# Folding a transform by halves and re-ordering three stages of a spectral-filter kernel

## The chip, the cores and the metric

One NeuronCore of one Trainium2 chip. The metric is device time in microseconds (us) of one execution. Times are quoted as the median of the runs of one round series. A profile shows one execution and has its own span, some 1.7 to 2.1 us shorter than the time of that same execution; stage lengths below are read from profiles.

## The reference

```python
def _A_ref(x, w_r, w_i):
    B, S, D = x.shape                        # 1, 2048, 576
    X = rfft2(x.astype(float32), axes=(-2, -1))
    X = X * (w_r + 1j * w_i)                 # weights 2048 x 289
    return irfft2(X, s=(S, D), axes=(-2, -1)).astype(bfloat16)

def _B_ref(x, w_gate, w_up, w_down):         # 576 -> 4608 -> 576
    return (gelu(x @ w_gate) * (x @ w_up)) @ w_down

h  = A_x + _A_ref(layernorm(A_x), w_r, w_i)
h2 = h + _B_ref(layernorm(h), w_gate, w_up, w_down)
```

Everything is bfloat16 in and out. The spectral filter (first line) takes the first 66 us of the kernel; the gated feed-forward (second line) takes the other 430 us.

## The kernel before

The work runs in four stages. The *table stage* computes the layernorm's statistics and multiplies x with a small table along the sequence, giving `U`. The *filter stage* runs, for each of 16 groups, a transform along d (`st_D`), a combination of even and odd parts (`st_U`), a second transform along the sequence (`st_B`), the product with the weights (`st_T`), its sums (`st_Z`), and a transform back (`st_V`). The *inverse stage* finishes the inverse transform and takes the second layernorm. Then comes the *feed-forward*. In the traces each engine does its own steps in the order in which the source issues them.

The parts (cuts are marked):

```python
    # ---- table stage: statistics of a tile by ScalarE are turned into a variance by VectorE
    def ln1_var(i):
        ...
            if c in ACT_TILES:
                P.op(DVE, lambda v, c=c: v.scalar_tensor_tensor(TM[:, 0, c:c + 1], SA[:, 0, c:c + 1], 1.0 / (D * D),
                                                                SA[:, 0, c:c + 1], op0=ALU.mult, op1=ALU.mult), ...)
        ...
                P.op(DVE, lambda v, c=c: v.scalar_tensor_tensor(MV1[:, c, 1:2], SA[:, 1, c:c + 1], 1.0 / D,
                                                                TM[:, 0, c:c + 1], op0=ALU.mult, op1=ALU.subtract), ...)

    TILES = (slice(0, 256, 2), slice(256, 512, 2), slice(1, 256, 2), slice(257, 512, 2), slice(512, D))
    def a_mm(i, k):                       # one matmul per tile of d and of the sequence
        ...
            P.op(PE, ... t.matmul(bank(b, 0, w, o, o + 128), XO[:, c, TILES[k]], ATS[:, c, :], start=True, stop=True), ...)

    # warm-up: loads ScalarE's table with the square root before anything else is there
    P.op(ACT, lambda a: a.activation(SA[:, 0, 0:1], EPT[:, 0:1], ACTF.Sqrt), ...)
    idle_mm(11, 0)
    act_sum(1)
    ...

    # ---- filter stage
    def st_D(i):
        ...                               # even-d result evicted by ScalarE to ES, odd-d result stays in PSUM
    def st_U(i):                          # VectorE: sum and difference from PSUM
        P.op(DVE, ... v.tensor_tensor(CUS[:, s3, :, 0:HK], e2, o2, op=ALU.add), ...)
        ...
        P.op(DVE, ... v.tensor_tensor(CUS[:, s3, :, K2 - 1:HK - 1:-1], e2[:, :, 0:HK - 1], o2[:, :, 0:HK - 1], op=ALU.subtract), ...)
    def st_B(i):                          # 6 matmuls a group, eviction by ScalarE to YS
        ...
    def st_T(i, t_, q0=0, q1=KW, hs=(0, 1)):   # two products a group, 580 elements each
        ...
    def st_V(i):                          # 3 column tiles a group: 128, 128 and the 33 that remain
        ...
    for i in range(NG):                   # GpSimd negates one plane of the weights
        P.op(POOL, lambda v, g=GORD[i]: v.tensor_scalar(WS[:, g, 0, :], WS[:, g, 2, :], -1.0, None, op0=ALU.mult), ...)
    for i in range(NG):
        st_D(i)
        st_U(i)
        if i >= 2:
            st_B(i - 2)
            st_T(i - 2, 0)
            st_T(i - 2, 1)
        if i >= 4:
            st_V(i - 4)
    ...
    # ---- inverse stage: the root of the variance is a power on GpSimd
        P.op(POOL, ... g.tensor_tensor(RS2[:, c0:c1], RS2[:, c0:c1], EXQ[:, c0:c1], op=ALU.pow), ...)
```

## Time and profile before

The kernel takes 498.09 us (498.00 to 498.15, 4 runs).

| Stage, cut at TensorE's first matmul of the next | us | TensorE busy | VectorE busy | ScalarE busy | GpSimd busy |
|---|---|---|---|---|---|
| wait for input | 3.67 | 2.37 | 0.00 | 1.49 | 2.91 |
| table | 16.28 | 13.14 | 14.65 | 15.53 | 4.79 |
| filter | 33.09 | 32.62 | 31.79 | 27.50 | 16.45 |
| inverse | 12.85 | 11.83 | 9.80 | 9.93 | 6.78 |
| feed-forward | 430.11 | 427.79 | 141.78 | 98.83 | 8.71 |

The table is this view of windows of the kernel before, whose row for 0.00 to 3.67 us is left out here. Its columns are the stretch in us, its length, then the busy time of each engine with the number of instructions in brackets, the granted clock, the DMA share and its rate.

```profile
core 0: us, PE busy (x) PEld busy (x) DVE busy (x) ACT busy (x) POOL busy (x), PEclk, DMA share, GB/s
3.67:19.95 16.28, 13.14 (x100) 7.35 (x98) 14.65 (x61) 15.53 (x45) 4.79 (x7) 0.90 0.95 284
19.95:53.04 33.09, 32.62 (x295) 26.42 (x296) 31.79 (x85) 27.50 (x49) 16.45 (x18) 1.00 0.52 161
53.04:65.89 12.85, 11.83 (x101) 8.52 (x102) 9.80 (x33) 9.93 (x22) 6.78 (x11) 1.00 1.02 349
65.89:496.00 430.11, 427.79 (x3825) 242.33 (x3824) 141.78 (x260) 98.83 (x177) 8.71 (x11) 1.00 0.13 38
```

A busy sum near the length of the stage says that an engine *could* be its limit. In the filter two engines qualify, TensorE and VectorE. Which of them is the limit is asked of the chain of waits, followed back from the end (window 36 to 53 us). Each row is a start, a length, and what the end had to wait for; the first line gives the shares of that window by line of the source.

```profile
by line: DVE TP L671 26.5%; PE PS L695 18.1%; issue 14.8%; DVE CUS L645 13.0%; DVE ZS L676 12.4%; DVE CUS L642 4.8%; PE PS L661 3.9%; DVE ZS L671 3.9%; DVE V L702 2.6%; PE PS L712 0.7%
...
41.42 0.74 DVE TP L671 x2
42.16 0.07 DVE CUS L642
42.23 0.22 issue
42.45 0.38 DVE ZS L676
42.83 0.44 DVE CUS L645
43.27 0.74 DVE TP L671 x2
...
```

Until 48.4 us every row is VectorE (DVE) or the gap between two of its instructions: products (TP), sums (ZS), and the sum and difference from PSUM (CUS), group after group. VectorE sets the pace of the filter. (The rows from 24 to 36 us are of the same kind.)

The costliest groups of the filter, from the profile's page (line, engine, operation, output and inputs, shape, count | busy us, mean ns | idle before, and what ended it):

```profile
L716 POOL TENSOR_SCALAR WS<-WS 128x290 bf16<-128x290 bf16 x16 | 15.9, 995 | 9.7 <-DMA WS<-in_A_w_i_dram 8.6
...
L671 DVE TENSOR_TENSOR TP<-YS,WS 128x580 bf16<-128x580 bf16 (+2 forms) x32 | 13.3, 453 | 0.3 <-issue 0.3
...
L664 ACT ACTIVATE YS<-PS 128x578 bf16<-128x578 f32 x16 | 10.5, 655 | 3.5 <-PE PS L661 3.1
L661 PE MATMUL PS<-CUS,BT 128*128 128x289 bf16 (+2 forms) x96 | 10.7, 247 | 0.3 <-DVE CUS L645 0.3
```

GpSimd needs 995 ns to negate 290 elements.

### The profile page before, as it was taken

How to read it: one execution, taken by the hardware profiler on the slowest of the kernel's cores; microseconds unless marked ns; L12 is line 12 of the kernel's file. 1: busy time of each engine (PE TensorE's matmuls, PEld its weight loads, DVE VectorE, ACT ScalarE, POOL GpSimd, SP SyncE). 2: the span in 40 equal slices, each digit the busy share in tenths (PEclk: the TensorE clock that was granted, in tenths of full speed). 3: DMA queues.
4: the chain of work that ended last, by engine and by line, in shares of the span. 5: the costliest groups of instructions: out<-in, count | busy, mean ns of one | idle time of the engine just before them, and what ended most of it. 6: DMA issues, size and time to landing. Idle time of an engine off the chain costs nothing.

```text
span 496.0 us, 9895 instructions
## 1 busy us (share of the span) xinstructions
PE 487.7 (98%) x4323; PEld 285.5 (58%) x4323; DVE 198.0 (40%) x436; ACT 153.3 (31%) x291; POOL 39.6 (8%) x52
## 2 busy tenths in 40 slices
PE   7999999999999999999999999999999999999998
PEld 2688744444488854444477744444677544444775
DVE  6899753343365543433311143433211233333111
ACT  7888763323322223323300023233100133233000
POOL 3644251000000020000000000000000000000000
PEclk9899999999999999999999999999999999999999
DMA  8765798511000052100000001100000000000000
GB/s 284 168 189 205 251 343 278 203 27 26 6 13 13 14 184 68 23 9 1 1 14 19 18 15 23 21 1 1 7 12 19 13 1 1 1 1 2 12 19 19
DMA packets 27163, 31.32 MB, mean 63 GB/s; under 512 B 11664, under 2 KB 19984, under 8 KB 27120
## 3 DMA queue, kind: packets, MB, share of 16 engines
q1 hardware_dynamic: 24224, 18.75, 13.1%
q0 software_dynamic: 2896, 11.95, 7.0%
q8 instruction: 34, 0.56, 0.5%
q14 instruction: 9, 0.07, 0.1%
HBM read 26.35 MB, written 2.36 MB: 58 GB/s over the span
## 4 chain that ended last, share of the span: by engine, by line
PE 89%; DVE 7%; issue 2%; DMA 1%; ACT 1%; POOL 0%; DVEq 0%
PE PS L910 56%; PE PS L960 29%; DVE TP L671 2%; DVE ST L472 1%; DVE CUS L645 1%; PE PS L927 1%; PE PS L775 1%; DVE ZS L676 1%; PE PS L695 1%; PE PS L814 1%; DMA XO<-in_A_x_dram 1%; PE PS L632 1%; DVE U L537 0%; DVE HN L842 0%; PE PS L941 0%
## 5 line engine op out<-in xcount | busy, mean ns | idle before, releaser
L910 PE MATMUL PS<-HT,WG 64*128 64x512 bf16 x2106 | 228.5, 376 | 0.0
L910 PEld LDWEIGHTS PS<-HT,WG 64*128 64x128 bf16 x2106 | 102.2, 94 | 124.8 <-issue 0.9
L920 DVE TENSOR_TENSOR AT<-GL,PS 128x512 bf16<-128x512 bf16 x144 | 99.1, 688 | 176.0 <-ACT GL L919 176.0
L919 ACT ACTIVATE GL<-PS 128x512 bf16<-128x512 f32 x144 | 86.0, 597 | 263.0 <-PE PS L910 249.6
L960 PE MATMUL PS<-WD,AT 128*128 128x288 bf16 (+2 forms) x1152 | 144.2, 286 | 0.0
L960 PEld LDWEIGHTS PS<-WD,AT 128*128 128x128 bf16 x1152 | 110.8, 98 | 30.7 <-ACT GL L919 1.3
L963 DVE TENSOR_TENSOR OS<-PS,XO 128x288 bf16<-128x288 f32 (+2 forms) x32 | 14.6, 458 | 100.3 <-PE PS L960 100.3
L910 PE MATMUL PS<-HT,WGX 64*128 64x512 bf16 x486 | 53.4, 376 | 0.0
L910 PEld LDWEIGHTS PS<-HT,WGX 64*128 64x128 bf16 x486 | 23.7, 94 | 28.8
L716 POOL TENSOR_SCALAR WS<-WS 128x290 bf16<-128x290 bf16 x16 | 15.9, 995 | 9.7 <-DMA WS<-in_A_w_i_dram 8.6
L632 PE MATMUL PS<-FT,U 128*128 128x290 bf16 x96 | 14.4, 287 | 0.4 <-DVE U L537 0.4
L805 ACT ACTIVATE JD<-XO 128x576 bf16<-128x576 bf16 x8 | 5.5, 683 | 28.5 <-DVE XO L944 28.5
L695 PE MATMUL PS<-VT,ZS 128*128 128x256 bf16 x102 | 13.5, 272 | 0.0
L671 DVE TENSOR_TENSOR TP<-YS,WS 128x580 bf16<-128x580 bf16 (+2 forms) x32 | 13.3, 453 | 0.3 <-issue 0.3
L833 POOL TENSOR_TENSOR RS<-RS,EXQ 128x2 f32<-128x2 f32 (+2 forms) x4 | 4.2, 1060 | 113.3 <-DVE RS L831 113.3
L708 ACT ACTIVATE V<-PS 128x768 bf16<-128x768 f32 x15 | 12.0, 811 | 0.9 <-PE PS L695 0.6
L664 ACT ACTIVATE YS<-PS 128x578 bf16<-128x578 f32 x16 | 10.5, 655 | 3.5 <-PE PS L661 3.1
L661 PE MATMUL PS<-CUS,BT 128*128 128x289 bf16 (+2 forms) x96 | 10.7, 247 | 0.3 <-DVE CUS L645 0.3
L632 PEld LDWEIGHTS PS<-FT,U 128*128 128x128 bf16 x96 | 9.2, 98 | 2.9 <-issue 0.6
L842 DVE TENSOR_SCALAR HN<-XO,TM,RS 128x576 bf16<-128x576 bf16 (+1 forms) x32 | 10.4, 372 | 0.4 <-POOL RS L833 0.4
L515 PE MATMUL PS<-ZD 128*128 128x512 bf16 x24 | 9.1, 537 | 1.3 <-POOL ZD L406 1.3
L695 PEld LDWEIGHTS PS<-VT,ZS 128*128 128x128 bf16 x102 | 9.2, 98 | 1.8 <-DVE ZS L676 0.2
(74 smaller groups left out, 199.4 us busy)
## 6 DMA issues: line engine op xcount, KB each, us to landing
WD<-in_B_w_down_dram POOLq DMA_DIRECT2D x9, 576.0 KB, 13.8
WG<-in_B_w_up_dram SPq DMA_DIRECT2D x4, 1152.0 KB, 6.5
WG<-in_B_w_gate_dram POOLq DMA_DIRECT2D x4, 1152.0 KB, 9.2
out_dram<-OS SPq DMA_DIRECT2D x30, 72.0 KB, 1.6
XO<-in_A_x_dram SPq DMA_DIRECT2D x3, 576.0 KB, 7.3
WGX<-in_B_w_up_dram SPq DMA_DIRECT2D x1, 1152.0 KB, 5.9
WGX<-in_B_w_gate_dram POOLq DMA_DIRECT2D x1, 1152.0 KB, 7.6
HT<-HN SPq DMA_TRANSPOSE x60, 2.4
```

The costliest lines, as they stand in the source:

```text
L632: P.op(PE, lambda t, b=b, o=o, dt=dt, us=us, g=g: t.matmul(bank(b, 0, 128, 0, 2 * HK), U[:, us, g, :, :], FT[:, o, dt, :], start=(dt == 0) ...
L661: P.op(PE, lambda t, b=b, tb=tb, pl=pl, q0=q0, q1=q1, m=m, s3=s3, sp_=sp_: t.matmul(bank(b, 0, 128, q0, q1), BT[:, sp_, tb, :], CUS[:, s3, ...
L664: P.op(ACT, lambda a, sl=sl, b0=b0: a.activation(YS[:, sl, :, 0:K2], banks(b0, 2, K2), ACTF.Copy), r=[("PS", b0), ("PS", b0 + 1)], w=[("Y" ...
L671: P.op(DVE, lambda v: v.tensor_tensor(out, YS[:, sl, :, q0:q1], WS[:, g, w_, q0:q1], op=ALU.mult), r=[("Y", sl), ("Wn", i), "Yz", "Zz"] + ...
L695: P.op(PE, lambda t, b=b, o=o, zp=zp, lhs=lhs, sp_=sp_, m=m, n=len(parts): t.matmul(bank(b, 0, 128, o, o + 256), lhs, VT[:, sp_, zp, :], s ...
L708: P.op(ACT, lambda a, dst=dst, src=src: a.activation(dst, src, ACTF.Copy), r=[("PS", bs[0]), ("PS", bs[2])], w=[("V", g, c) for c in range ...
L716: P.op(POOL, lambda v, g=GORD[i]: v.tensor_scalar(WS[:, g, 0, :], WS[:, g, 2, :], -1.0, None, op0=ALU.mult), r=[k for k in wkeys[0 if 1 <= ...
L910: op = P.op(PE, lambda t, h0=h0, kt=kt, wt=wt, b=b, s=(not second and j == 0), e=(second and j == n - 1): t.matmul(bank(b), wg_tile(slot)[ ...
L919: P.op(ACT, lambda a: a.activation(GL[:, s2, :], bank(b0), ACTF.Gelu_apprx_tanh), r=[("PS", b0)], w=[("GL", s2)])
L920: P.op(DVE, lambda v: v.tensor_tensor(AT[:, f, :], GL[:, s2, :], bank(b0 + 1), op=ALU.mult), r=[("GL", s2), ("PS", b0 + 1)], w=[("AT", f)])
L960: P.op(PE, lambda t, b=b, d0=d0, d1=d1, f=f, p=p: t.matmul(bank(b, 0, 128, 0, d1 - d0), AT[:, f, 128 * p:128 * p + 128], WD[:, f, d0:d1], ...
L963: P.op(DVE, lambda v, b=b, d0=d0, d1=d1, p=p, c=c: v.tensor_tensor(OS[:, p % 2, d0:d1], bank(b, 0, 128, 0, d1 - d0), XO[:, c, d0:d1], op=A ...
```

## The change

The intent, part by part:

- **Fold by halves, half-sample shift, k2 = 0 left out.** The layernorm takes the mean out along d, so frequency 0 of that transform is zero, and 288 frequencies remain. For odd and even frequencies the transform needs only x[d] − x[d + 288] and x[d] + x[d + 288]. TensorE forms both while it computes the table products, by accumulating two matmuls; the difference needs a negated second half, `XN`, which GpSimd makes. With that, the filter's 32 VectorE sums and differences (`st_U`) go, and `st_B` needs 4 matmuls a group instead of 6. ScalarE evicts the transform and interleaves odd and even frequencies while it writes.
- **Products in one instruction** of 1152 elements a group, with the data read twice.
- **Tails in one matmul.** The last 32 of 288 columns of four groups are put side by side in `ZR` and transformed by one pair of matmuls (`st_R`), then copied into `VR`, which has to be zero elsewhere.
- **New orders** of the table, filter and inverse stages, given as strings; six smaller groups in the table stage instead of five. The warm-up square root is gone. The power on GpSimd becomes a square root on ScalarE and a reciprocal.

```diff
+GROUPS = ((0, 2), (2, 4), (4, 7), (7, 10), (10, 13), (13, 16))
+SEQ1 = """k14 B0 S3 B1 v0 q0 ... E2A E3D n1 B7 q2 E4A n2 c2 ... """.split()
+SEQF = """D0 D1 D2 B0 B1 T0 T1 ... V4 D11 Z7 R1 Z8 B10 D12 T9 ... R4 V15 R3""".split()
+RENG = [['dve', 'dve', 'act', 'dve'], ['dve', 'dve', 'dve', 'act'], ['act', 'dve', 'dve', 'dve'], ['dve', 'act', 'dve'], ['dve']]
...
-    P.op(POOL, lambda g: g.memset(YS[:, :, :, K2:KW], 0.0), w=["Yz"])
-    P.op(POOL, lambda g: g.memset(ZS[:, :, :, K2:ZW], 0.0), w=["Zz"])
+    P.op(POOL, lambda g: g.memset(VR[:, :, :, :, :], 0.0), w=["Vz"])
...
+    def a_mm(i):
+        ...
+                    x2 = XN[:, c, d0:d0 + 128] if k % 2 else XO[:, c, 288 + d0:416 + d0]
+                    parts = [(XO[:, c, d0:d0 + 128], 0, 128, True, False), (x2, 0, 128, False, True)]
...
+    def x_neg(i):
+        P.op(POOL, lambda g: g.tensor_scalar(XN[:, c0:c1, :], XO[:, c0:c1, 288:D], -1.0, 1.0, op0=ALU.mult, op1=ALU.mult), ...)
-    P.op(ACT, lambda a: a.activation(SA[:, 0, 0:1], EPT[:, 0:1], ACTF.Sqrt), r=["EPT"], w=[("SA0", 0)])
...
-    def st_U(i):
-        ...                                    # two VectorE instructions a group
+    def st_D(i, eng=ACT):
+        ...
+        ev(eng, CUS[:, s3, :, :].rearrange("p a (j r) -> p r a j", r=2), banks(b0, 2, 2 * HK).rearrange("p r (a j) -> p r a j", a=2), ...)
+    def st_B(i, eng=ACT):
+        for b, tabs in ((b0, (0, 1)), (b0 + 1, (1, 2))):
+            for m, tb in enumerate(tabs):
+                P.op(PE, ... t.matmul(bank(b, 0, 128, 0, KW), BT[:, sp_, tb, :], CUS[:, s3, m, :], start=(m == 0), stop=(m == 1)), ...)
+        ev(eng, YS[:, sl, :, :], banks(b0, 2, KW), ...)
+    def st_T(i, q0=0, q1=KW, hs=(0, 1)):
+        ...
+        y4 = YS[:, sl, :, q0:q1].unsqueeze(1).to_broadcast([128, 2, 2, q1 - q0])
+        P.op(DVE, lambda v: v.tensor_tensor(TP[:, sl, :, :, q0:q1], y4, w4, op=ALU.mult), ...)
+    def st_R(q, engs, b=7):
+        ...                                    # two matmuls for four groups' tails, then a copy per group on engine engs[j]
...
-        P.op(POOL, lambda v, ...: v.tensor_scalar(WS[:, g, 0, :], WS[:, g, 2, :], -1.0, None, op0=ALU.mult), ...)
+        P.op(POOL, lambda v, ...: v.tensor_scalar(WS[:, g, 0, :], WS[:, g, 2, :], -1.0, 1.0, op0=ALU.mult, op1=ALU.mult), ...)
...
-        P.op(POOL, ... g.tensor_tensor(RS2[:, c0:c1], RS2[:, c0:c1], EXQ[:, c0:c1], op=ALU.pow), ...)
+        P.op(ACT, ... a.activation(RS2[:, c0:c1], RS2[:, c0:c1], ACTF.Sqrt, bias=EPT[:, 0:1]), ...)
+        P.op(DVE, ... v.reciprocal(RS2[:, c0:c1], RS2[:, c0:c1]), ...)
```

In the order strings a letter is a step and the number its group: in `SEQF`, D, B, T, Z, V are the steps above and R is a tail; in `SEQ1`, n is the negation, v and q the variance and its root, x the scaled table, M the matmuls and E their evictions.

## The prediction

> **What bounds the kernel now.** Cut at its seams, the span of 496.0 us (windows view) is: wait for the first input 3.7; table stage 16.3 (3.67 to 19.95); filter 33.1 (to 53.04); inverse transform with second layernorm 12.9 (to 65.95); feed-forward 430.05, in which TensorE is busy 427.7 and waits 0.3 us. The change touches almost only the first 66 us; the feed-forward cannot give anything.
>
> Table stage: the chain of waits runs through VectorE (statistics, scaled tables, copies), busy 14.65 of 16.3 us; ScalarE 15.5. Filter: VectorE is busy 31.8 of 33.1 and is what the chain names, but TensorE is nearly full too: an estimate from columns at 2.4 GHz plus 2.5 ns per matmul (the Trainium skill, "TensorE: Matmul & The Clock Gate", the section on 56 against 53.3 ns; the trace agrees: 648 feed-forward matmuls, two at a time, in 70.0 us, so 216 ns a pair) gives 30.9 us. ScalarE 27.5.
>
> **Filter after.**
> - TensorE: D 96 matmuls of 288 columns, B 64 instead of 96 (7.8 us against 8.0, same columns), V 64 instead of 102, plus 10 tail matmuls: 27.7 us instead of 30.9.
> - VectorE: the 32 sums and differences from PSUM (14.3 us busy) go. The products become 16 of 1152 elements, about 0.67 us each if the broadcast keeps two elements a cycle; sums 0.34 + 0.13; 12 tail copies of about 0.36: about 22.5 us.
> - ScalarE: now 32 evictions of 576 (655 ns busy, about 0.57 in pitch), 15 of 512 (0.52), 6 small: about 28.0 us instead of 25.9 in pitch. It becomes the bound, with TensorE just under it. The step-two write of the D eviction I take as free; the strided V eviction fits the same line as the plain ones (768 in 811 ns).
>
> With 0.8 us before the first eviction and a tail, I expect about 30.3 us: 2.8 saved.
>
> **Table stage after.** TensorE issues 160 matmuls of 128 columns (80 before), about 9 us, but drops little filler; not binding. VectorE about 15.4 us of work, 0.5 more. ScalarE about 16 with a second table load (1.28 us, since the warm-up square root is gone). GpSimd gets a 4096-element memset (3.5 us, from 1.8 for 2048) and 4608 elements of negation before the matmuls can run; the present negation takes 0.995 us for 290, and at that rate it would bind. I assume that the two-operation form is faster. Smaller last groups help. Net +0.5 us.
>
> **Inverse stage after.** Same matmuls; GpSimd's power (0.72 to 0.82 us on the chain) becomes a ScalarE root and a reciprocal (0.3 + 0.17), one VectorE step (0.17) goes; TensorE idles about 2 us here now. About 0.7 us saved.
>
> **Feed-forward after.** Two square roots among the gelus cost four table loads of 1.28 us on ScalarE (the Trainium skill, "ScalarE: Activation LUTs", says a switch costs about 2.7 us with its drain; the trace shows 1.28 and no gap behind it), hidden by four PSUM pairs of about 1.95 us each. Zero.
>
> **Time.** 498.1 + 0.5 - 2.8 - 0.7 = 495.1 us; 8 in 10: 492.6 to 498.3. Faster by over 2%: 0.01; within 2%: 0.98; slower by over 2%: 0.01.
>
> **Right or wrong by.** Filter 29.5 to 31.5 us, its chain through ScalarE and TensorE instead of VectorE; product near 0.7 us; D eviction near 0.65; table stage 16 to 18; inverse stage near 12.2; feed-forward 430.0 without TensorE waits at the table loads.
>
> **What would make it wrong.** Negation on GpSimd at 3 ns an element (table stage +5 us, total near 500); the product at one element a cycle (1.2 us, filter bound by VectorE again); a slow strided eviction; or a filter packed better than I grant, with a shorter table stage, giving 492.

## The result and the profile after

The changed kernel takes **497.07 us** (497.05 to 497.13, 4 runs) against 498.09 us before, a ratio of 0.998 with a 95% interval of 0.9963 to 0.9997: the same within 2%, and about 1.0 us faster. The forecast was 3.0 us of gain; a third of it came.

The windows of the changed kernel, cut at the same seams:

```profile
3.75:21.80 18.05, 13.74 (x176) 9.42 (x174) 16.86 (x65) 15.44 (x45) 11.61 (x13) 1.00 0.85 260
21.80:52.75 30.95, 28.88 (x238) 22.18 (x235) 24.79 (x61) 29.77 (x54) 9.91 (x19) 1.00 0.55 168
52.75:65.18 12.43, 11.89 (x100) 8.59 (x101) 9.98 (x34) 10.58 (x25) 8.01 (x11) 1.00 1.02 357
65.18:495.30 430.12, 427.73 (x3824) 247.37 (x3824) 142.05 (x260) 104.26 (x182) 2.60 (x4) 1.00 0.13 38
```

| Stage | before | after | change | forecast |
|---|---|---|---|---|
| wait for input | 3.67 | 3.75 | +0.08 | 0 |
| table | 16.28 | 18.05 | +1.77 | +0.5 |
| filter | 33.09 | 30.95 | −2.14 | −2.8 |
| inverse | 12.85 | 12.43 | −0.42 | −0.7 |
| feed-forward | 430.11 | 430.12 | +0.01 | 0 |

The changes add up to −0.70 us, the difference of the two spans (496.0 and 495.3); another 0.3 us lies outside the spans, and nothing here explains it. The largest error is the table stage, 1.3 us; the second is the filter, 0.7.

**The table stage.** The first thing that happens late is ScalarE's first square root. Its timeline (start, length, engine, line, operation; what ended an idle time in brackets), before and then after:

```profile
5.70 0.28 ACT L489 ACTIVATE RS<-MV,EPT 128x2 f32<-128x2 f32 x1
```

```profile
4.48 0.68 ACT L455 ACTIVATE JNK<-XO 128x576 bf16<-128x576 bf16 x1 [2.46 <-DMA XO<-in_A_x_dram]
5.07 0.19 ACT L455 ACTIVATION_READ_ACCUMULATOR JNK<-XO 128x1 f32 x1
5.26 1.28 ACT L481 ACT_TABLE_LOAD   x1
6.55 0.29 ACT L481 ACTIVATE RS<-MV,EPT 128x2 f32<-128x2 f32 x1
```

The warm-up root is gone, so the root's table is loaded where the root is needed, in line with what waits for it: 1.28 us, and the first root starts at 6.55 instead of 5.70.

The second thing is odd. Here are VectorE, GpSimd and ScalarE of the changed kernel around 10 us, from its timeline:

```profile
9.70 0.10 DVE L470 SCALAR_TENSOR_TENSOR TM<-SA 128x1 f32<-128x1 f32 x1
9.73 0.20 DVE L473 BATCH_NORM_AGGREGATE MV<-ST 128x2 f32<-128x12 f32 x1
9.91 0.86 DVE L476 SCALAR_TENSOR_TENSOR MV<-SA,TM 128x1 f32<-128x1 f32 x1
...
9.85 0.91 POOL L536 TENSOR_SCALAR XN<-XO 128x864 bf16<-128x864 bf16 x1 [0.15 <-POOL XN L536]
...
10.80 0.30 ACT L481 ACTIVATE RS<-MV,EPT 128x3 f32<-128x3 f32 x1 [0.90 <-DVE MV L476]
```

An instruction on one element takes 0.86 us where its twin took 0.10. It starts just after GpSimd began a negation (9.85) and ends when the negation ends (10.76 and 10.77). ScalarE's next root waits 0.90 us for it. The same happens at 13.49 and 18.35 (0.46 us each, each ending with a negation).

**The filter.** The groups of the page that answer to those shown of before:

```profile
L595 DVE TENSOR_TENSOR TP<-YS,WS 128x1152 bf16<-128x1152 bf16 (+2 forms) x17 | 12.1, 736 | 4.7 <-ACT YS L566 4.4
L566 ACT ACTIVATE CUS<-PS 128x576 bf16<-128x576 f32 x16 | 12.9, 834 | 0.5 <-PE PS L575 0.4
L566 ACT ACTIVATE YS<-PS 128x576 bf16<-128x576 f32 x16 | 10.3, 658 | 0.3 <-DVE TP L595 0.2
L585 PE MATMUL PS<-CUS,BT 128*128 128x288 bf16 x64 | 10.1, 286 | 0.0
```

Two evictions of the same size from PSUM differ by 0.18 us (834 against 658 ns): the one that interleaves while it writes is slower. And the chain of waits that leads to the end of the filter (window 36 to 53 us again) still runs through VectorE. This view can follow it back to 43.6 us only:

```profile
by line: DVE TP L595 15.9%; PE PS L611 9.4%; issue 7.9%; DVE ZS L601 7.5%; DVE VR L566 5.3%; DVE ZR L604 3.3%; ACT V L566 2.3%; PE PS L621 1.9%; PE PS L683 1.7%
...
47.85 0.68 DVE TP L595
48.53 0.02 issue
48.56 0.04 DVE ZS L601
48.59 0.31 issue
48.90 0.18 DVE ZR L604
49.08 0.68 DVE TP L595
49.76 0.02 issue
49.79 0.44 DVE ZS L601
...
```

VectorE's first product starts at 25.75, because it needs the first group's two transforms and two evictions; its last sum ends at about 50.2. So the stage is a head of 3.95 us, some 24.5 us in which VectorE waits only 1.7 us in all, and a tail of 2.5 us (21.80 to 25.75 to 50.22 to 52.75). In the middle TensorE waits once for long, at the tail product of groups 4 to 7:

```profile
39.62 0.38 PE L621 MATMUL PS<-VT,ZR 128*128 128x256 bf16 x2 [1.40 <-DVE ZR L604]
```

### The profile page after: what moved, and what is told of

The parts are those of the page before. It is cut to its first block, busy times and chain, and to the rows that moved or that the text cites. A ratio compares the mean times of both kernels' runs of the same rounds, so it can differ in the third digit from the quotient of the medians.

```text
span 495.3 us, 9884 instructions
## 1 busy us (share of the span) xinstructions
PE 484.7 (98%) x4338; PEld 288.4 (58%) x4338; DVE 193.7 (39%) x417; ACT 161.3 (33%) x304; POOL 35.2 (7%) x52
## 3 DMA queue, kind: packets, MB, share of 16 engines
q1 hardware_dynamic: 24224, 18.68, 12.9%
## 4 chain that ended last, share of the span: by engine, by line
PE 88%; DVE 2%; issue 0%; ACT 0%; DVEq 0%
PE PS L823 57%; PE PS L873 29%; PE PS L840 1%; PE PS L683 1%; PE PS L722 1%; DVE TP L595 1%; DVE XO L725 0%; PE PS L854 0%; PE PS L611 0%; DVE ZS L601 0%; DVE VR L566 0%; DVE HN L756 0%; PE PS L776 0%; DVE ZR L604 0%; DVE TM L733 0%
## 5 line engine op out<-in xcount | busy, mean ns | idle before, releaser
L522 PE MATMUL PS<-ATS,XO 128*128 128x128 bf16 (+1 forms) x128 | 10.5, 221 | 4.3 <-DVE ATS L496 1.9
L595 DVE TENSOR_TENSOR TP<-YS,WS 128x1152 bf16<-128x1152 bf16 (+2 forms) x17 | 12.1, 736 | 4.7 <-ACT YS L566 4.4
L575 PE MATMUL PS<-FT,U 128*128 128x288 bf16 x96 | 13.9, 286 | 0.0
L566 ACT ACTIVATE CUS<-PS 128x576 bf16<-128x576 f32 x16 | 12.9, 834 | 0.5 <-PE PS L575 0.4
L522 PEld LDWEIGHTS PS<-ATS,XO 128*128 128x128 bf16 (+1 forms) x128 | 7.5, 97 | 7.3 <-DVE ATS L496 2.7
L464 DVE BATCH_NORM_STATS2 ST<-XO 128x6 f32<-128x288 bf16 x24 | 9.2, 439 | 3.7 <-DMA XO<-in_A_x_dram 3.7
L566 ACT ACTIVATE YS<-PS 128x576 bf16<-128x576 f32 x16 | 10.3, 658 | 0.3 <-DVE TP L595 0.2
L585 PE MATMUL PS<-CUS,BT 128*128 128x288 bf16 x64 | 10.1, 286 | 0.0
L857 DVE SCALAR_TENSOR_TENSOR XO<-PS,XO 128x576 bf16<-128x576 f32 x8 | 6.1, 757 | 8.0 <-PE PS L854 8.0
L566 ACT ACTIVATE V<-PS 128x512 bf16<-128x512 f32 (+1 forms) x17 | 9.1, 584 | 0.2 <-PE PS L611 0.2
```

Source lines behind the costliest of these rows:

```text
L464: P.op(DVE, lambda v, c=c, h=h: v.bn_stats(ST1[:, c, h, :], XO[:, c, 288 * h:288 * h + 288]), r=[("X", c)], w=[("ST1", c, h)])
L522: P.op(PE, lambda t, b=b, lhs=lhs, p0=p0, p1=p1, s=s, e=e, o=o, c=c: t.matmul(bank(b, p0, p1, o, o + 128), lhs, ATS[:, c, :], start=s, sto ...
L566: fn = (lambda v: v.tensor_copy(dst, src)) if eng == DVE else (lambda a: a.activation(dst, src, ACTF.Copy))
L575: P.op(PE, lambda t, b=b, m=m, us=us, o=o, g=g: t.matmul(bank(b, 0, 128, 0, 2 * HK), U[:, us, g, :, :], FT[:, 3 * o + (2 if us == 4 else u ...
L585: P.op(PE, lambda t, b=b, tb=tb, m=m, s3=s3, sp_=sp_: t.matmul(bank(b, 0, 128, 0, KW), BT[:, sp_, tb, :], CUS[:, s3, m, :], start=(m == 0) ...
L595: P.op(DVE, lambda v: v.tensor_tensor(TP[:, sl, :, :, q0:q1], y4, w4, op=ALU.mult), r=[("Y", sl), ("Wn", i)] + wkeys[0 if 1 <= g < 9 else ...
```

## The experiments

Eighteen kernels ran. All differ from the changed kernel by the edits told, all gave correct results except one, and none moved the feed-forward's length. "D start" is TensorE's first matmul of the filter (before 19.95, after 21.80), "filter" is the length from there to the first matmul of the inverse stage (before 33.09, after 30.95). Letters for theories in a quoted expectation belong to that quotation.

### The table stage: is it the table load, or GpSimd holding VectorE?

Theory one: the second table load delays the first root. Theory two: VectorE's instructions with two tensor operands in SBUF are held while GpSimd runs. The Trainium skill, "SBUF — State Buffer", the section "Who interferes with whom", says that a VectorE instruction with two SBUF inputs contends with a GpSimd instruction that reads SBUF, because its second input comes through a read interface that the two share. The rival of both: the folded matmuls and the smaller groups simply need the time.

**Warm-up root put back.**

```diff
+    P.op(ACT, lambda a: a.activation(SA[:, 0, 0:1], EPT[:, 0:1], ACTF.Sqrt), r=["EPT"], w=[("SA0", 0)])
     ENG = {"A": ACT, "D": DVE, "P": POOL}
```

> The changed kernel with the warm-up square root of the kernel before put back, so that one activation table serves the whole table stage instead of two loads (the second, 1.28 us, stands at 5.26 us between the first statistics and the first root, and VectorE waits 0.67 us behind it). Theory A (the first chain is late because of that load, and the lateness travels to the end of the stage): the first root at about 5.6 instead of 6.55 us, first matmul of the d transform at about 21.0 instead of 21.80, whole kernel 496.3. Rival B (later waits on VectorE and ScalarE work set the end of the stage, the early delay is swallowed): first root earlier by the same, but the d transform still at 21.6 to 21.8 and the whole at 496.9 to 497.1.

Measured: 496.75 us, ratio to before 0.9974 (0.9957 to 0.9991). One table load; the reciprocal after the first root comes 0.83 us earlier (6.05 instead of 6.88), but D starts at 21.35, only 0.45 us earlier. About half of the 0.83 is taken up on the way, and the filter behind it takes 31.10 us, 0.15 more.

**Only one SBUF tensor as input.** The same two one-element steps, with the second operand as a per-partition scalar.

```diff
-v.scalar_tensor_tensor(TM[:, 0, c:c + 1], SA[:, 0, c:c + 1], 1.0 / (D * D), SA[:, 0, c:c + 1], op0=ALU.mult, op1=ALU.mult)
+v.tensor_scalar(TM[:, 0, c:c + 1], SA[:, 0, c:c + 1], 1.0 / (D * D), SA[:, 0, c:c + 1], op0=ALU.mult, op1=ALU.mult)
-v.scalar_tensor_tensor(MV1[:, c, 1:2], SA[:, 1, c:c + 1], 1.0 / D, TM[:, 0, c:c + 1], op0=ALU.mult, op1=ALU.subtract)
+v.tensor_scalar(MV1[:, c, 1:2], SA[:, 1, c:c + 1], 1.0 / D, TM[:, 0, c:c + 1], op0=ALU.mult, op1=ALU.subtract)
```

> The changed kernel with the eight one-element variance steps on VectorE written with one tensor input and a pointer scalar instead of two tensor inputs. Theory A (three of these steps, 0.86, 0.46 and 0.46 us long for one element, are held while GpSimd runs a negation[...]): each takes about 0.1 to 0.2 us, VectorE gains about 1.3 us, the d transform starts at 20.8 to 21.2 us, the whole at 496.1 to 496.5. Rival B (any VectorE instruction is slowed while GpSimd reads, or the steps wait for a semaphore): the same three steps stay long, start of the d transform 21.7 to 21.9, whole 497.0 to 497.2.

The timeline of this run around 10 us:

```profile
9.70 0.16 DVE L470 TENSOR_SCALAR TM<-SA 128x1 f32<-128x1 f32 x1
...
9.97 0.21 DVE L476 TENSOR_SCALAR MV<-SA,TM 128x1 f32<-128x1 f32 x1
...
9.86 0.91 POOL L536 TENSOR_SCALAR XN<-XO 128x864 bf16<-128x864 bf16 x1 [0.15 <-POOL XN L536]
```

The negation is where it was, and the step beside it now takes 0.21 us instead of 0.86. The new form is slower by itself (0.16 against 0.10), so the gain can only come from not being held. This agrees with the section named above. D starts at 20.72, 1.08 us earlier. Time 496.33 us, ratio 0.9975 (0.9959 to 0.9991). The profiled run was the longest of the four (497.95, the others 496.18 to 496.42); TensorE waited 1.95 us at the tail product of groups 4 to 7 and then its granted clock fell to 0.50 (40 to 42 us). So of this profile only the table stage is used.

**No negation at all (wrong result).** The second half is read unnegated, so sums stand where differences belong.

```diff
-x2 = XN[:, c, d0:d0 + 128] if k % 2 else XO[:, c, 288 + d0:416 + d0]
+x2 = XO[:, c, 288 + d0:416 + d0]
-P.op(POOL, lambda g: g.tensor_scalar(XN[:, c0:c1, :], XO[:, c0:c1, 288:D], -1.0, 1.0, ...))
+pass
```

> Wrong result on purpose: the differences become sums, so that GpSimd negates nothing in the table stage (six instructions, 4.9 us, gone) and TensorE has the same matmuls. If the negations hold VectorE (theory A) the same gain as with one tensor input, about 0.6 to 1.0 us at the start of the d transform; if the first scaled tables and negations delay TensorE as well, more, up to 1.5 us. Rival B (the doubled matmuls or the ScalarE evictions alone make the stage longer): less than 0.3 us.

Measured: D starts at 20.34, 1.46 us earlier, with every folded matmul still in place. This refutes the rival that the folding's TensorE work costs the time: what costs it is the negation on GpSimd, though TensorE hardly waits for its results. (The 0.39 us that remain against the kernel before are less than what the warm-up root gave.) VectorE is busy 15.42 us in this table stage, against 16.86 in the changed kernel.

The time is 496.33 us (ratio 0.9968), so only half of the earlier start reaches the end: the filter takes 31.69 us, 0.74 more, and TensorE's wait at the tail product of groups 4 to 7 grows by as much, from 1.40 to 2.14 us. One thing in the middle of the filter does not move with its start: GpSimd waits for the second half of the weights to arrive by DMA, and negates them from 33.30 us on here, from 32.60 in the changed kernel. Whether that takes back the gain was not tested.

### The filter: is it ScalarE's slower eviction?

Theory: the interleaving write costs 16 × 0.18 = 2.9 us of ScalarE, which the forecast names as the new limit. Three ways to put the interleave elsewhere.

**Interleave in TensorE's read.**

```diff
-CUS[:, s3, :, :].rearrange("p a (j r) -> p r a j", r=2)     # eviction of D
+CUS[:, s3, :, :].rearrange("p a (r j) -> p r a j", r=2)
-CUS[:, s3, m, :]                                            # moving operand of B
+CUS[:, s3, m, :].rearrange("p (r j) -> p j r", r=2)
```

> The changed kernel with the eviction of the d transform writing contiguous halves, and the next matmul reading its moving operand interleaved instead. Theory A (the write with a step of two makes this eviction 0.83 us instead of about 0.65, and ScalarE bounds the filter): eviction 0.65 us, ScalarE 2.4 us less, filter stage 30.95 down to 29.3 to 30.0 us if TensorE reads the interleaved operand at full rate, whole 496.1 or less. Rival B (two banks in one read, not the write, are slow): eviction stays at 0.83. If TensorE pays for the step, its matmuls of 288 columns take clearly longer than 0.12 us each in a row and the filter gains nothing or loses.

```profile
L585 PE MATMUL PS<-CUS,BT 128*128 128x288 bf16 x64 | 19.7, 435 | 0.0
L566 ACT ACTIVATE CUS<-PS 128x576 bf16<-128x576 f32 x16 | 10.4, 651 | 1.1 <-PE PS L575 0.4
```

The eviction falls to 651 ns, so the cost was the stepped write. But B's matmuls go from 286 to 435 ns, and the kernel takes 504.21 us (ratio 1.0126). TensorE pays far more for the same rearrangement.

**Interleave in ScalarE's read of PSUM,** one step later, in the eviction of B.

```diff
-ev(eng, YS[:, sl, :, :], banks(b0, 2, KW), ...)
+ev(eng, YS[:, sl, :, :].rearrange("p a (j r) -> p a j r", r=2), banks(b0, 2, KW).rearrange("p a (r j) -> p a j r", r=2), ...)
```

(and the contiguous eviction of D as above)

> The changed kernel with the eviction of the d transform writing contiguous halves, the next matmul reading them contiguously, and the interleave done by the next eviction, which then reads PSUM with a step of 144 elements and writes contiguously. Theory A (what costs 0.15 to 0.18 us per eviction is the two-byte write with a step of two, not the number of rows): the first eviction 0.65 us; the second stays at 0.65 if ScalarE reads PSUM freely, filter 29 to 30 us, whole about 495.5 to 496.2. Rival B (any step costs ScalarE, read or write): the cost moves to the second eviction, which takes 0.8 us or more, and the whole is 496.9 to 497.5 or worse.

Measured: 496.92 us, ratio 0.9981 (0.9966 to 0.9995). D's evictions take 657 ns, B's 653: the stepped read of PSUM is free for ScalarE, whose D evictions, as a group, are busy 2.4 us less (10.5 against 12.9). The filter stays at 30.93 us. Its window, to be set beside that of the changed kernel (ScalarE's is the fourth busy time: 28.51 us against 29.77. It falls by less than 2.4 because neighbouring evictions overlap, and time in which two of them run is counted once):

```profile
21.80:52.73 30.93, 28.69 (x238) 22.24 (x235) 24.94 (x61) 28.51 (x54) 9.44 (x19) 1.00 0.56 171
```

**ScalarE's sum is not what bounds the stage.**

**Interleave in TensorE's write to PSUM.**

```diff
-t.matmul(bank(b, 0, 128, 0, KW), BT[...], CUS[:, s3, m, :])
+t.matmul(bank(b, 0, 128, 0, KW).rearrange("p (j r) -> p r j", r=2), BT[...], CUS[:, s3, m, :].rearrange("p (r j) -> p r j", r=2))
```

> The same, but the interleave is done by TensorE's write: each matmul behind the d transform writes its 288 columns to every second PSUM column in two runs; all evictions are contiguous. Theory A: both evictions 0.65 us; if TensorE writes PSUM with a step at full rate (0.12 us each) the filter takes 29 to 30 us and the whole 495.5 to 496.2; if it pays as for the interleaved read (0.27 us each) the whole is near 504.

Measured: 502.23 us (ratio 1.0088), both evictions at 650 ns, B's matmuls at 438 ns. TensorE pays again.

**Two evictions of D (groups 1 and 2) on VectorE,** to let the first product start earlier.

```diff
-            st_D(i)
+            st_D(i, DVE if i in (1, 2) else ACT)
```

> The changed kernel with the evictions of groups 1 and 2 of the d transform on VectorE, which is idle then (it waits 3.5 us for the first products). Theory A (ScalarE, 29.8 of 30.95 us busy, bounds the filter): first Y eviction about 0.5 us earlier, ScalarE 1.4 us less, filter 29.8 to 30.4 us, whole 496.2 to 496.6. Rival B (TensorE and the chain through VectorE in the middle of the filter set its length): filter 30.8 to 31.0, whole 496.9 to 497.2.

Measured: 497.21 us (ratio 0.9986, 0.997 to 1.0003); ScalarE has 1.1 us less, VectorE 1.6 more, the filter takes 31.09 us. No gain.

### All at once, and the same hold a second time

**A combination:** the two table-stage repairs, the two evictions on VectorE, the tail product R1 two matmul groups later, and the zeroing of `VR` moved behind the last negation.

```diff
-SEQF = "... D11 Z7 R1 Z8 B10 D12 T9 ..."
+SEQF = "... D11 Z7 Z8 B10 D12 R1 T9 ..."
-    P.op(POOL, lambda g: g.memset(VR[:, :, :, :, :], 0.0), w=["Vz"])     # at its old, early place
+    P.op(POOL, lambda g: g.memset(VR[:, :, :, :, :], 0.0), w=["Vz"])     # after the table stage's last negation
```

> The sum of the repairs: one table load, one-tensor variance steps, the memset of the tail table moved behind the negations on GpSimd, evictions 1 and 2 on VectorE, and the tail matmul of groups 4 to 7 three steps later in TensorE's order (it waits 1.4 us there for VectorE, 1.95 us when the filter starts earlier). If the parts add: start of the d transform about 20.0 us (1.8 earlier), filter 29.8 to 30.5 us, whole 494.3 to 495.2. If the second half of the filter weights and the negation of it on GpSimd (from 32.6 to 33.5 us whatever the start) hold the middle, the filter grows by what the table stage gives and the whole stays at 495.5 to 496.2.

It became slower: 498.83 us (ratio 1.0019), D starting at 24.32; its filter takes 30.25 us. The timeline says why, VectorE first, then GpSimd:

```profile
18.16 3.10 DVE L495 TENSOR_SCALAR ATS<-ATB,RS 128x128 bf16<-128x128 bf16 x3
...
17.62 3.52 POOL L545 MEMSET VR<- 128x4096 bf16 x1
```

Three scalings that take 0.58 us together in the changed kernel took 3.10, and end with the zeroing (21.26 and 21.14). These have one SBUF tensor input, and a zeroing reads nothing. So one input is no protection for every instruction. The same section of the Trainium skill covers it: `tensor_scalar`, the operation of these scalings, can enter a mode that needs the port pair shared with GpSimd, whoever issues first has the pair for the whole instruction, and the other blocks. That it is this mode which these scalings were in, no view of a trace shows; the hold and its end the trace does show. For TensorE it was dear: it was idle for 2.65 us, and its granted clock was 0.62 between 20 and 24 us.

### The order of the tail product

**R1 behind B10** (one matmul group later, nothing else changed), and then **together with the interleave in the read of PSUM**.

```diff
-SEQF = "... D11 Z7 R1 Z8 B10 D12 T9 ..."
+SEQF = "... D11 Z7 Z8 B10 R1 D12 T9 ..."
```

> The changed kernel with one token moved in the filter's order: the tail matmul of groups 4 to 7 goes behind the next matmul group instead of before it. Theory C (the filter's length is set by TensorE standing 1.4 us at this tail matmul, for sums that VectorE delivers late, while freeing ScalarE changed nothing in the two runs that did it): the wait of 1.4 us disappears, filter 29.6 to 30.3 us instead of 30.95, whole 496.2 to 496.6. Rival A (ScalarE, 29.8 of 30.95 us busy, is the limit): filter 30.7 to 31.0, whole 496.9 to 497.1.

> The tail matmul moved and the contiguous d eviction with the interleave read from PSUM together. If both limits lie close to each other (wait at the tail first, ScalarE right behind it), the eviction that gave nothing alone now gives 0.3 to 1 us more than the move alone: filter 28.8 to 29.7, whole 495.3 to 496.1. If only the wait mattered: the same as the move alone within 0.2 us.

Measured: 496.66 us (0.9973) with a filter of 30.46, and 496.51 us (0.9971) with 30.38. The wait of TensorE at R1 falls from 1.40 to 0.84 us, and the stage by 0.49. The relief of ScalarE adds 0.08, which is too little to be told from noise.

**Everything, with the zeroing behind the last scaling** (so that no scaling can be held), without and with the two evictions on VectorE.

```diff
-    P.op(POOL, lambda g: g.memset(VR[:, :, :, :, :], 0.0), w=["Vz"])
+    P.op(POOL, lambda g: g.memset(VR[:, :, :, :, :], 0.0), r=[("ATS", NT - 1)], w=["Vz"])    # after the table stage
```

> All repairs but the evictions on VectorE: one table load, one-tensor variance steps, contiguous d eviction, tail matmul moved, and the memset of the tail table behind the last scaled table, where it can no longer hold VectorE (in the combined run before it held three scalings of 0.2 us for 3.1 us). Start of the d transform 20.2 to 20.7 us, filter 29.0 to 30.2, whole 493.9 to 495.3. If an earlier start is eaten in the middle of the filter (weights of its second half come at a fixed time): filter near 30.5 and whole 495.3 to 495.8.

> The same with the evictions of groups 1 and 2 of the d transform on VectorE. VectorE idles at the head of the filter, so the head is 0.4 us shorter: 0.2 to 0.4 us less than without if the middle does not take it back, otherwise the same within 0.1 us.

Measured: 495.52 us (0.995, 0.9935 to 0.9965) and 495.47 us (0.9948). D starts at 20.19 and 20.24, 1.6 us earlier than in the changed kernel: the table-stage loss is back. The filter takes 30.84 and 30.96. It lost what R1's move had gained. Two causes are open. The zeroing is one: it pushes GpSimd's negations of the weights to 22.4 to 27.4 us, into VectorE's first products, where a pair took 1.86 us (1.43 in the changed kernel). The earlier start itself is the other: without the negation the filter grew by 0.74 us though no zeroing was moved, and here too the second half of the weights is negated no earlier than before (from 32.59 and 33.05 us). No run separates the two.

### Is VectorE the limit, or the split between two engines?

By now the natural reading was that VectorE's sum alone bounds the filter: in the version just told it had no gap longer than 0.2 us between 28.9 and 49.9 us. Test: move work off it.

**Six of the nine tail copies that VectorE makes for groups 0 to 11, moved to ScalarE** (with R1 later and the interleave in PSUM).

```diff
-RENG = [['dve', 'dve', 'act', 'dve'], ['dve', 'dve', 'dve', 'act'], ['act', 'dve', 'dve', 'dve'], ...]
+RENG = [['act', 'dve', 'act', 'act'], ['act', 'dve', 'act', 'act'], ['act', 'dve', 'act', 'act'], ...]
```

> The run with the tail matmul moved and the contiguous d eviction, plus six of the twelve small tail copies (32 partitions, 0.42 us each) moved from VectorE to ScalarE. Theory D (the filter is VectorE's: it cannot start before the first products, about 4.2 us after the stage begins, and is then busy without a gap to the end; freeing ScalarE or moving one tensor wait gives little): VectorE 2.5 us less, filter 30.4 down to 28.2 to 29.5 us, whole 494.5 to 495.6. Rival (ScalarE or TensorE is the limit by now): ScalarE gets 1.7 us more, filter 30.2 us or longer, whole 496.4 or more.

Measured: 496.9 us (0.9978), filter 30.77, *worse* than the 30.38 of the same version with no copy moved. VectorE is relieved of 1.8 us, and waits for ScalarE's evictions instead: three copies in a row, 1.15 us, stand in ScalarE's queue before an eviction that the next product needs. The chain of waits (window 36 to 53 us) now runs through ScalarE:

```profile
by line: ACT V L566 37.6%; ACT YS L566 21.8%; ACT CUS L566 11.2%; issue 10.0%; ACT VR L566 5.5%; PE PS L575 4.3%; PE PS L683 3.1%; PE PS L585 3.0%; PE PS L611 2.6%; PE PS L621 2.2%
```

So in this version VectorE is not the limit; ScalarE has taken its place. That VectorE was the limit as long as no copy was moved, this run does not refute.

**The same with the table stage repaired,** without and with the two evictions on VectorE. The zeroing goes back to its early place, written as half as many 4-byte zeros. The Trainium skill, "VectorE: DVE Perf Modes", the section on zero memsets issued as uint32, states this for VectorE; on GpSimd the 4096 elements took 3.52 us as bfloat16 and 1.81 us as 2048 float32.

```diff
-g.memset(VR[:, :, :, :, :], 0.0)
+g.memset(VR[:, :, :, :, :].rearrange("p a b c d -> p (a b c d)").bitcast(F32), 0.0)
-g.memset(U[64:128, 4, :, :, :], 0.0)
+g.memset(U[64:128, 4, :, :, :].rearrange("p a b c -> p (a b c)").bitcast(F32), 0.0)
```

> All repairs (one table load, one-tensor variance steps, contiguous d eviction, tail matmul moved, six tail copies on ScalarE) and the two large memsets on GpSimd issued as 4-byte zeros, half the elements, at their old place, so that they neither delay the first negation nor run beside VectorE's scalings. Start of the d transform 20.0 to 20.4 us; with theory D filter 28.2 to 29.5, whole 492.8 to 494.5; without it 495.2 to 495.6 as in the two runs of all repairs before.

> The same with the evictions of groups 1 and 2 on VectorE, which idles at the head: theory D wants the first products earlier, so 0.2 to 0.5 us less than without; if ScalarE has become the limit through the copies, likewise less. No gain if TensorE (27.7 us of work) is the limit by then.

Measured: 495.34 us (0.9945) and 495.49 us (0.9948); filter 30.78 and 30.77, D start 20.32 and 20.29. Here the earlier start cost the filter nothing (30.77 with D at 21.80).

**Three copies moved instead of six,** with the two evictions on VectorE.

```diff
-RENG = [['dve', 'dve', 'act', 'dve'], ['dve', 'dve', 'dve', 'act'], ['act', 'dve', 'dve', 'dve'], ...]
+RENG = [['act', 'dve', 'act', 'dve'], ['dve', 'act', 'dve', 'act'], ['act', 'dve', 'act', 'dve'], ...]
```

> The same with three copies moved instead of six. Theory D: between the run with none and the run with six, that is 0.5 to 1.2 us slower than with six, unless ScalarE limits with six, in which case it is equal or faster.

Measured: **494.68 us** (494.34 to 495.08), ratio to before 0.9934 (0.9919 to 0.9948); filter 29.92, D start 20.10. But this version has many edits. Two last runs took it apart.

**The three filter edits alone on the changed kernel** (R1 later, interleave in PSUM, three copies moved), table stage untouched:

> The kernel after with three edits of the filter stage alone: the second tail product one place later, the interleave in the PSUM read of the second transform's eviction, and three of the six tail copies moved from VectorE to ScalarE. Table stage untouched, so first D matmul at 21.80. Theory S (the two eviction engines must be balanced; neither alone bounds the stage): filter 29.7 to 30.1 us, below both neighbours, 30.38 with no copy moved and 30.77 with all six moved. Rival theory T (the gain of the best version's filter came from its repaired table stage or from two evictions put on VectorE, not from the balance): filter 30.4 or more.

**The best version without the two evictions on VectorE:**

> The best version without its two first-transform evictions on VectorE, everything else kept. If these two evictions matter, filter about 30.3 to 30.8 instead of 29.92 (with all six copies moved they made no difference, 30.78 against 30.77); if the balance of the copies is what matters, filter within 0.2 of 29.92, and the median within 0.3 of 494.68. First D matmul at 20.1 to 20.3 either way.

Measured: 496.08 us (0.9962, 0.9947 to 0.9977) with a filter of 29.93; and 494.59 us (494.35 to 494.89; 0.9931, 0.9915 to 0.9948) with a filter of 30.15. In the first, D starts at 21.80 as it must. So the filter's gain needs neither the repaired table stage nor the two evictions, and the rival falls. The first differs from R1 behind B10 with the interleave in PSUM by the three copies alone, and its filter is 0.45 us shorter (29.93 against 30.38): with no copy moved, VectorE's work did hold the filter. In the second, the evictions look worth 0.2 us in the profile (the expected limit of 0.2 was missed by 0.03) and nothing in the median; its four runs spread by 0.54 us. The window of the filter, and the chain of waits to its end (window 36 to 53 us), for the version with the three edits alone:

```profile
21.80:51.73 29.93, 28.68 (x238) 22.30 (x235) 23.98 (x58) 29.09 (x57) 9.91 (x19) 1.00 0.58 175
```

```profile
by line: ACT V L566 17.6%; PE PS L575 17.3%; PE PS L611 12.9%; PE PS L585 11.5%; DVE TP L595 10.4%; ACT YS L566 7.9%; PE PS L683 7.9%; DVE ZS L601 5.3%; PE PS L621 3.5%; issue 3.2%; DVE ZR L604 2.7%; DVEq L282 0.4%
...
42.62 0.49 PE PS L585 x4
43.11 0.87 PE PS L611 x8
43.98 0.73 PE PS L575 x6
44.72 0.22 PE PS L621 x2
...
```

Set this beside the chain of the changed kernel. There, VectorE's products and sums filled the rows from 43.6 to 50.2 us. Here VectorE's rows end at 39.3 us, those from 39.4 to 47.1 are TensorE's transforms back to back, and the last 4.5 us are ScalarE's evictions. This is the chain that the prediction had named for the changed kernel, "through ScalarE and TensorE instead of VectorE", and it comes with the length that it had forecast, or a little less (29.93 against 30.3).

In one table, filter lengths with only filter edits. Each is of one profile; the four times of each of these kernels spread by 0.02 to 0.23 us, so differences of 0.1 us are not to be read:

| Edit on the changed kernel | filter, us |
|---|---|
| none | 30.95 |
| D evictions 2.4 us shorter (interleave in PSUM) | 30.93 |
| ScalarE relieved by 1.1 us (two evictions to VectorE) | 31.09 |
| tail product later | 30.46 |
| tail product later, ScalarE relieved | 30.38 |
| the same, and three copies from VectorE to ScalarE | 29.93 |
| the same, and six copies from VectorE to ScalarE | 30.77 |

## Why the prediction was right or wrong

It forecast 495.1 us and a gain of 3.0; the gain was 1.0. The time lies in its range and is within 2% of before, as it said, but the gain was mis-sized threefold. Term by term:

- **Table stage, forecast +0.5, measured +1.77. This is the step that failed most.** The prediction saw the second table load and counted it into ScalarE's sum ("about 16"), and it saw GpSimd's negation and asked only whether it would be *fast* enough. It was: 0.91 us for 864 elements. In its sum, the term that was mis-sized is "VectorE about 15.4 us of work, 0.5 more": VectorE was busy 16.86 us, 2.2 more, and 15.42 us in the run without the negation. What the sum left out is *where* the negation and the table load stand. The table load stands in front of the first root, which everything waits for; putting the warm-up back gave 0.45 us. The negation runs beside VectorE, and VectorE's two-input steps stop for as long as it runs; giving these steps one tensor input gave 1.08 us, and removing the negation altogether 1.46. With both repairs, and other edits beside them, the filter starts at 20.1 to 20.3 us, 1.5 to 1.7 earlier: 0.15 to 0.4 us later than in the kernel before, where the forecast had said 0.5.
- **Filter, forecast −2.8 (to 30.3), measured −2.14 (30.95). The step that failed is "It becomes the bound, with TensorE just under it"**, said of ScalarE. Taking 2.4 us off ScalarE's D evictions (1.26 us off its busy time as a whole) changed nothing. VectorE was put at 22.5 us and not looked at again; it measured 24.8, and behind a head of 3.95 us and before a tail of 2.5 us that is the whole stage. The head was forecast as "0.8 us before the first eviction", but VectorE cannot start before a *second* eviction. Yet VectorE is not the only limit either: with six copies moved away the stage was longer than with none. Two engines hand work to each other, each doing its steps in the order of the source, and of the versions tried the stage got its forecast length only when a tail product stood later, ScalarE was relieved by the interleave in PSUM, and the copies were split between both. Only splits of none, three and six were tried. That three is best of these because of where each copy stands in ScalarE's queue is argued from one timeline, not shown.
- **"The step-two write of the D eviction I take as free": wrong in size** (834 against 651 to 658 ns, 2.9 us of ScalarE in all), **without effect on the time where it alone was mended** (filter 30.93 against 30.95).
- **The product at 0.67 us: right where VectorE is undisturbed** (0.68 in the chain from 47.85 on), 0.74 in the mean. While GpSimd negates the second half of the weights (32.6 to 38.0 us) a product takes up to 0.97 and the small sum 0.40 instead of 0.18. That agrees with the cause found in the table stage; no run with this negation removed was made.
- **GpSimd's two-operation negation is fast: right** (519 ns for 288 elements against 995 ns for 290; 0.43 against 0.94 us where VectorE does not stretch them).
- **TensorE's filter work of 27.7 us: not refuted.** The best filter takes 29.9 us with 28.7 us of TensorE busy time, in which pipelined matmuls overlap, so the work itself is not read off.
- **Inverse stage, forecast −0.7, measured −0.42.** The direction was right; no run tested why the rest is missing. The prediction also read its seam 0.06 us late (65.95 for 65.89).
- **Feed-forward, forecast 0, measured +0.01: right.** The extra table loads hide.

The best version (warm-up root, one tensor input, 4-byte zeroing, R1 later, interleave in PSUM, three copies moved) runs at 494.59 us, 0.9931 of before, and beats both kernels. The change's idea was worth the forecast 3 us; two thirds of it were lost to how the pieces stood beside each other.

## What to carry to other kernels

A sum of busy time per engine gives a floor, not a time: ask for each new instruction what stands right behind it, and on which *other* engine its mere presence can stop work. Put new GpSimd work where VectorE does nothing that shares its ports, or give VectorE forms that do not share them, and look in the trace for short instructions that suddenly end together with a long one on GpSimd. When relieving the suspected engine changes nothing and relieving its neighbour makes things worse, try the balance and the order between them before deciding that the stage is full.

## What the Trainium skill lacked or had wrong

- "SBUF — State Buffer", "Who interferes with whom": it had the decisive rule, and the table stage agrees with it. It lacks an example of the damage to tiny instructions, which no sum of elements suggests: a one-element step took 0.86 us instead of 0.10 beside a 0.91 us negation, and three scalings 3.10 instead of 0.58 us beside a zeroing of 3.52 us.
- The same section says "fully blocks" of the two-port modes, and gives no size for products with two SBUF inputs. Where such products and negations follow one another the runs show that each stretches the other: a negation took 0.43 us before VectorE's first product and up to 0.91 beside products, and eight of them 5.44 instead of 4.02 us; a pair of products took 1.64 instead of 1.43 us. Waiting for the rest of the other's instruction would be enough for that, so it does not contradict the section.
- "ScalarE: Activation LUTs", "What ACT_TABLE_LOAD costs": 1283 ns for the load agrees (1.28 us), but the drain of about 1380 ns that it adds does not show here: the load started at 5.26 and the next instruction at 6.55.
- "SBUF — State Buffer", the note on cachelines under "Door 1: The DMA port swizzle", gives a stride of a few 16-bit elements as free. For ScalarE's write with a step of two elements the runs show 834 against 651 to 658 ns for 576 elements. Its note that a non-contiguous PSUM pattern slows matmuls agrees (438 against 286 ns); that ScalarE reads PSUM with such a step for nothing (653 against 658 ns) stands on none of the pages consulted.
- "GPSIMD Engine Reference": no entry for the two forms of the same negation, 995 ns (one operation, 290 elements) and 519 ns (two operations, 288 elements). Form and length changed together, so the runs do not tell which of them does it.
- "VectorE: DVE Perf Modes", zero memsets as uint32: it speaks of VectorE alone; on GpSimd the time also went by elements (3.52 us for 4096, 1.81 us for the same bytes as 2048).
